# The low part of a gated layer's weights: two 64-row products in the two halves of the array, in groups of two steps

## The chip, the cores and the metric

One core of one Trainium2 chip runs the whole program. The metric is the time of one execution on the device in microseconds; of several executions the median counts. TensorE (PE) multiplies, VectorE (DVE), ScalarE (ACT) and GpSimd (POOL) do the rest on chip, and SyncE (SP) issues most transfers.

## The reference

Three stages follow each other: a gated linear attention, a mixture of eight experts with two experts per token, and a gated dense layer. The change is in the last stage, for 1536 tokens of 320 columns:

```python
def _moe2_ref(x, w_gate, w_val, w_out):
    g = x @ w_gate                                # 320 -> 1536
    silu = g * (1.0 / (1.0 + np.exp(-g)))
    val = x @ w_val                               # 320 -> 1536
    return (silu * val @ w_out).astype(np.float32)   # 1536 -> 320

def reference(**kwargs):
    ...
    attn_out = _attn_ref(**attn_kwargs)
    ...
    x = _moe_ref(x=x, **moe_kwargs)
    return _moe2_ref(x=x, **moe2_kwargs)
```

## The kernel before

The second layer (the last stage) takes the tokens in thirds (`q`, 512 tokens each) and the 1536 hidden columns in twelve steps (`f`, 128 columns each): 36 steps, in the order of the loop at L1105. Numbers are multiplied as float32r, which keeps fewer bits than float32, so each operand is split into a high and a low part and a product is made of three: high by high, high by low, low by high.

The 320 input columns are three pieces: two of 128, and the last of 64. `x2part` transposes the tokens piece by piece (`px`, L834), and makes for the first two pieces the tiles `x2h` (high) and `x2l` (low). The last piece is laid twice into 128 rows, and its tile `xr` (`x2r` in the trace) has the high part in rows 0 to 63 and the low part in rows 64 to 127. The weights' last piece also stands twice in its 128 rows, so one product with `xr` makes high by high and high by low together. The product of the weights' low part with `xr` uses all 128 rows as well.

`passes` (L646) issues the eight matmuls of one sum: three for each of the first two pieces, two for the last. `l1` (L843) calls it twice in each step, for the gate (`pg`) and the value (`pv`), each into a bank of PSUM of its own. The banks come from the ring `A` of four, which `px` uses too. Then ScalarE makes the sigmoid `sg` of `pg` (L852), VectorE multiplies `pg` by `sg` (L853) and that by `pv` (L854) into `u`. `l1_split` splits `u` into `uh` (ScalarE, L862) and `ul` (VectorE, L863). `l2` (L865) multiplies these by the output weights: twelve matmuls of 320 columns per step (L874) into four banks (`py`, rings `Y` and `O`) that sum over the twelve steps of a third; after the last step ScalarE and VectorE take turns in evicting the four banks into tiles `osb`, and SyncE stores them. The `osb` tiles use the buffers of `u` and `sg`, two of each.

The order on each engine is the order of the code. A step is: `l1`; two pieces of weights of the next groups of columns, split by ScalarE (L545) and VectorE (L546), as long as there are any (16 in the first third); in the first third `combine`, in which VectorE adds gathered expert rows (L803) and ScalarE copies the last columns (L798); `l1_split`; `l2` of two steps before (`LAG`); after steps 8, 9 and 10 of the first two thirds one piece of the next third's `x2part`.

Of the kernel before, what the change touches and what calls it, by code (L numbers as in the profile page):

```python
# [7 lines left out]
F32 = mybir.dt.float32  # L8
F32R = mybir.dt.float32r
# [22 lines left out]
CVN = 44  # L32
# attention: chunks after which a batch of tokens is routed, lag of the copies to DRAM and of the first loads
BT = (0, 2, 4, 6, 8, 10, 12)
# [3 lines left out]
XI = 10  # L38
# experts: steps of a unit that prepare the next unit's tokens, units whose sums lie in the other banks,
# step at which the first full unit's tokens are loaded, units whose last columns are doubled on ScalarE  # L40
XK = (4, 5, 6)
OB = (1, 9)
XL = 10
DU = (0, 1, 2)
# columns of the moving operands: heads per product of the attention, columns of the gate's weights
IW = 3
GW = 128
# gathers of expert rows in the last units (CA) and in the second layer's first steps
CA = (1, 1, 1, 1, 1, 1, 1, 2, 1, 1, 0, 0, 0)
XS = 5  # L50
CM2 = (2, 2, 2, 1, 2, 2, 2, 1, 3, 2, 2, 1)
# after the attention: 0 is a step of the experts, k that many steps of the last routing
SEQ = (0, 0, 6, 2, 0, 2, -99)
# pieces of weights that are split per step
RT = (1, 1, 2, 1, 2, 1, 2, 1, 0, 0, 2, 1, 1, 1, 2, 1, 1, 1, 2, 1, 1, 1, 2, 1, 1, 1, 3, 1, 1, 1, 2, 1, 1, 1, 1, 2, 2, 0, 3, 2, 1, 1, 1, 2, 2, 1, 3, 1, 1, 1, 1, 2, 2, 1, 2, 1, 1, 2, 1, 2, 2, 1, 2, 2, 1, 2, 1, 2, 2, 1, 2, 0, 1, 2, 1, 2, 2, 1, 2, 1)
AN = 6
AT = (5,9,7,11)
AG = (5, 11, 8)
# programs of the start, the second, the middle and the last chunks (codes in ON_START and ON_CHUNK;
# in START those of ON_CHUNK are shifted by 256)  # L60
START = 'gffhqkQlffffffff1cfrffff2dffsffffxoOffSffff34WKfTy5Gmfnafwfe6ffffŇŷ7ũŗŋűzųŮŭŶť'
# [29 lines left out]
def kernel(ctx, tc, qk, kvh, og, gates, cst, wgn, noise, w1, w2, w13, w2o, out):  # L91
# [10 lines left out]
    def bankA(name):  # L102
        return ps.tile([128, 512], F32, name=name, tag="A")
# [9 lines left out]

    # ---------------- persistent tiles and constants
    CW = cst.shape[1]
# [40 lines left out]

    # ---------------- attention
    mos = ExitStack()
# [219 lines left out]

    # ---------------- routing
    def route(t0, t1):  # L380
# [124 lines left out]

    # ---------------- weight stream: load, split into two float32r parts
    EX = [(e, 0) for e in SPLIT] + [(e, 0) for e in FULL] + [(e, 1) for e in SPLIT]
# [41 lines left out]

    # ---------------- float64 weights to float32, through DRAM  # L550
    CV = []
# [42 lines left out]

    # ---------------- experts
    XG, XT, HT, YP = {}, {}, {}, {}
# [48 lines left out]

    def passes(ps_ap, wt, wl, cols, xt, n):  # L646
        xh, xl, xr = xt
        seq = []
        for k in range(2):
            c = slice(k * 512 + cols, k * 512 + cols + 128)  # L650
            seq += [(wt[:, c], xh[:, k, 0:n]), (wt[:, c], xl[:, k, 0:n]), (wl[:, c], xh[:, k, 0:n])]
        c = slice(1024 + cols, 1024 + cols + 128)
        seq += [(wt[:, c], xr[:, 0:n]), (wl[:, c], xr[:, 0:n])]
        for i, (a, b) in enumerate(seq):
            pe.matmul(ps_ap, a, b, start=(i == 0), stop=(i == len(seq) - 1))  # L655

# [53 lines left out]

    # ---------------- tokens beyond the capacities
    def overflow_counts():
# [66 lines left out]

    # ---------------- second layer  # L780
    X2 = {}
# [37 lines left out]
    def x2prep(q):  # L819
        pool = m2 if q == 1 else xp[0]  # L820
        xh = pool.tile([128, 2, 512], F32R, name="x2h", bufs=1)
        xl = pool.tile([128, 2, 512], F32R, name="x2l", bufs=1)
        xr = pool.tile([128, 512], F32R, name="x2r", bufs=1)
        X2[q] = (xh, xl, xr)

    def x2part(q, k0, k1):
        if q not in X2:
            x2prep(q)
        xh, xl, xr = X2[q]
        for k in range(k0, k1):  # L830
            ready(q, k)
            p = bankA("px2")
            for a in range(4):
                pe.transpose(p[:, a * 128:(a + 1) * 128], x[:, q * 4 + a, k * 128:(k + 1) * 128], ident)  # L834
            if k < 2:
                s.activation(xh[:, k, :], p, AF.Copy)
                v.tensor_tensor(out=xl[:, k, :], in0=p, in1=xh[:, k, :], op=OP.subtract)
            else:
                s.activation(xr, p, AF.Copy)
                v.tensor_tensor(out=xr[64:128], in0=p[64:128], in1=xr[64:128], op=OP.subtract)  # L840

    UT, OP_ = {}, {}

    def l1(q, f):
        st = GU[f // 4]
        pg = bankA("pg2")
        passes(pg, *WT[st[0]], (f % 4) * 128, X2[q], 512)
        pv = bankA("pv2")
        passes(pv, *WT[st[1]], (f % 4) * 128, X2[q], 512)
        sg = m2.tile([128, 512], F32, name="sg")  # L850
        u = m2.tile([128, 512], F32, name="u")
        s.activation(sg, pg, AF.Sigmoid)  # L852
        v.tensor_tensor(out=sg, in0=pg, in1=sg, op=OP.mult)  # L853
        v.tensor_tensor(out=u, in0=pv, in1=sg, op=OP.mult)  # L854
        UT[q, f] = u

# [8 lines left out]
    def l2(q, f):  # L865
        if f == 0:
            OP_[q] = banksY(4)
        wh, wl = WT[GU[f // 4][2]]
        c = slice((f % 4) * DM, (f % 4 + 1) * DM)
        uh, ul = UT[q, f]  # L870
        for a in range(4):
            t = slice(a * 128, (a + 1) * 128)
            for i, (x_, w) in enumerate(((uh, wh), (uh, wl), (ul, wh))):
                pe.matmul(OP_[q][a][:, 0:DM], x_[:, t], w[:, c], start=(f == 0 and i == 0), stop=(f == 11 and i == 2))  # L874
            if f == 11:
                o = m2.tile([128, 512], F32, name="osb", tag=("u", "sg")[a % 2])[:, 0:DM]
                if a % 2 == 0:
                    s.activation(o, OP_[q][a][:, 0:DM], AF.Copy)
                else:
                    v.tensor_copy(o, OP_[q][a][:, 0:DM])  # L880
                r0 = (q * 4 + a) * 128
                sy.dma_start(out[r0:r0 + 128, :], o)

    # ---------------- experts
    steps = [(n, f) for n in range(len(EX)) for f in range(8)]
# [71 lines left out]

    # ---------------- attention schedule
    def clear():
# [143 lines left out]
    bg = [p for k in (1, 2) for u in GU[k] for p in wpieces(u)]  # L1103
    steps = [(q, f) for q in range(3) for f in range(12)]
    for i, (q, f) in enumerate(steps):  # L1105
        l1(q, f)
        for _ in range(2):
            if bg:
                bg.pop(0)()
        if q == 0:  # L1110
            combine(CM2[f])
        l1_split(q, f)
        if i >= LAG:
            l2(*steps[i - LAG])
        if f in (8, 9, 10) and q < 2:
            x2part(q + 1, f - 8, f - 7)
    for q, f in steps[-LAG:]:
        l2(q, f)

# [64 lines left out]
```

## Time and profile before

| | us |
|---|---|
| median of 3 runs | 567.21 (565.85 to 569.94) |
| profiled execution, span from first to last instruction | 577.4 |
| profiled execution, outside the span | not listed on the page |
| second layer in it, first pg matmul to last py matmul | 375.5 to 573.7 |

The span and all the rows below are of the one profiled execution. The page gives busy times as sums over the whole program; what a stretch is limited by is read from the rows of that stretch, above all from which engine's wait ends last in it.

### The profile page before, as it was taken

Reading aid. Unit: us, or ns where it says so; the run is one execution under the profiler, and the core shown is the slowest. Engines: PE = TensorE matmul, PEld = TensorE weight load, DVE = VectorE, ACT = ScalarE, POOL = GpSimd, SP = SyncE. Lnnn points to the kernel's source line nnn. Section 1 sums busy time; section 2 is a strip of 40 time slices with the busy share of each in tenths; the row PEclk is TensorE's granted clock in tenths of the full one; section 3 lists DMA queues with packets and bytes.
Section 4 is the critical chain, followed back from the end, with each engine's and each line's share of the span. In section 5 each row is a group of like instructions: output and inputs, shape, how many; then the busy total and the mean of one; then the engine's idle time right before and its main releaser. Section 6 shows DMA issues by size and latency. Waiting matters only on the chain. (4 is left out here: it accounts for less than half of the span.)

```text
span 577.4 us, 9288 instructions
## 1 busy us (share of the span) xinstructions
PE 541.0 (94%) x3337; PEld 488.4 (85%) x3337; DVE 383.6 (66%) x884; ACT 276.9 (48%) x599; POOL 176.6 (31%) x207
## 2 busy tenths in 40 slices
PE   8998878859799989999999969999999999999997
PEld 4677878758689979999999969988888888888886
DVE  5447887887558988889989847877753434434433
ACT  5345644323356667778776836555332222222221
POOL 4034666555412735353533315433100000000000
PEclk7559887879979989999999989999999999999999
DMA  8748664402755777888987747744000100010001
GB/s 243 164 139 261 204 210 143 146 23 104 218 197 170 262 266 255 298 300 286 310 306 253 266 162 256 231 151 157 23 2 0 47 1 0 2 45 1 0 1 45
DMA packets 36055, 88.72 MB, mean 154 GB/s; under 512 B 10640, under 2 KB 16944, under 8 KB 36000
## 3 DMA queue, kind: packets, MB, share of 16 engines
q1 hardware_dynamic: 30320, 75.08, 39.5%
q0 software_dynamic: 3360, 8.38, 4.8%
q10 hardware_dynamic: 2320, 4.58, 2.3%
q8 instruction: 28, 0.46, 0.3%
q14 instruction: 27, 0.22, 0.1%
HBM read 72.80 MB, written 15.21 MB: 152 GB/s over the span
## 5 line engine op out<-in xcount | busy, mean ns | idle before, releaser
L692 PE MATMUL py<-wV,h 128*128 128x320 f32 (+1 forms) x624 | 108.5, 315 | 3.1 <-ACT ysb L703 2.3
L692 PEld LDWEIGHTS py<-wV,h 128*128 128x128 f32 (+1 forms) x624 | 97.2, 188 | 4.8 <-ACT ysb L703 2.8
L655 PE MATMUL ph<-xh,wU 128*128 128x416 f32 (+1 forms) x320 | 91.2, 335 | 4.9 <-issue 4.1
L585 POOL TENSOR_TENSOR cq<-cq,csg 128x512 f32<-128x512 f32 (+1 forms) x27 | 39.2, 1453 | 93.0 <-ACT cq L584 60.9
L655 PEld LDWEIGHTS ph<-xh,wU 128*128 128x128 f32 x320 | 59.2, 193 | 7.5 <-issue 4.4
L874 PE MATMUL py<-wV,uh 128*128 128x320 f32 x288 | 63.9, 309 | 0.0
L853 DVE TENSOR_TENSOR sg<-pg,sg 128x512 f32<-128x512 f32 x36 | 24.9, 691 | 58.1 <-ACT sg L852 58.1
L546 DVE TENSOR_TENSOR wU<-stg,wU 128x512 fp32r<-128x512 f32 x72 | 52.4, 753 | 6.2 <-ACT wU L545 5.8
L852 ACT ACTIVATE sg<-pg 128x512 f32<-128x512 f32 x36 | 21.5, 598 | 65.5 <-PE pg L655 60.0
L862 ACT ACTIVATE uh<-u 128x512 fp32r<-128x512 f32 x36 | 22.8, 632 | 61.6 <-DVE u L854 60.7
L655 PE MATMUL ph<-xl,wU 128*128 128x416 f32 (+1 forms) x160 | 52.1, 325 | 0.0
L874 PEld LDWEIGHTS py<-wV,uh 128*128 128x128 f32 x288 | 49.5, 188 | 2.8
L655 PE MATMUL pg<-x2h,wU 128*128 128x512 f32 x144 | 51.2, 396 | 0.0
L655 PE MATMUL pv<-x2h,wU 128*128 128x512 f32 x144 | 50.5, 391 | 0.0
L545 ACT ACTIVATE wU<-stg 128x512 fp32r<-128x512 f32 x78 | 46.4, 624 | 7.0 <-DVE yt L701 4.8
L664 ACT ACTIVATE h<-ph 128x416 fp32r<-128x416 f32 (+1 forms) x80 | 35.7, 447 | 26.2 <-PE ph L655 20.0
L874 PE MATMUL py<-wV,ul 128*128 128x320 f32 x144 | 44.4, 309 | 0.0
L546 DVE TENSOR_TENSOR wV<-stg,wV 128x640 fp32r<-128x640 f32 x42 | 37.0, 890 | 3.5 <-ACT wV L545 3.4
L612 POOL DMA_INDIRECT xgt<-xd,xi x32 | 32.6, 1019 | 21.0 <-PEq L733 6.4
L655 PE MATMUL ph<-xr,wU 128*128 128x416 f32 (+1 forms) x160 | 38.7, 324 | 0.0
L791 POOL DMA_INDIRECT gy<-yg,ig__89 x24 | 25.1, 1046 | 44.0 <-DVE x L803 15.5
L863 DVE TENSOR_TENSOR ul<-u,uh 128x512 fp32r<-128x512 f32 x36 | 24.9, 691 | 19.9 <-ACT uh L862 19.9
(177 smaller groups left out, 1123.7 us busy)
## 6 DMA issues: line engine op xcount, KB each, us to landing
stg<-in_w_dram SPq DMA_DIRECT2D x20, 768.0 KB
stg<-in_w_dram SPq DMA_DIRECT2D x20, 640.0 KB
cw<-in_w_dram SPq DMA_DIRECT2D x18, 512.0 KB
gbt<-gp SPq DMA_DIRECT2D x10, 512.0 KB
f<-cq SPq DMA_DIRECT2D x18, 256.0 KB
stg<-f SPq DMA_DIRECT2D x6, 768.0 KB
kvt<-in_kvh_dram SPq DMA_DIRECT2D x12, 324.0 KB
QK<-in_qk_dram SPq DMA_DIRECT2D x24, 160.0 KB
```

The lines of the kernel that those rows point to most:

```text
L545: s.activation(hi[:, c], ST[u][:, c], AF.Copy)
L546: (g if lo_pool[0] else v).tensor_tensor(out=lo[:, c], in0=ST[u][:, c], in1=hi[:, c], op=OP.subtract)
L585: g.tensor_tensor(out=q, in0=q, in1=sg, op=OP.mult)
L612: g.indirect_dma_start(out=XG[n][0:nr // m, c, 0:DM], out_offset=None, in_=xd[0:S] if n < len(SPLIT) else xd, in_offset=bass.IndirectOffse ...
L655: pe.matmul(ps_ap, a, b, start=(i == 0), stop=(i == len(seq) - 1))
L664: s.activation(h[:, 0:C], p[:, 0:C], AF.Relu)
L692: pe.matmul(yp[0:nr, 0:DM], x_, w, start=st and i == 0, stop=sp and i == 2)
L791: g.indirect_dma_start(out=y, out_offset=None, in_=yg[0:NR0] if j < NC else yg, in_offset=bass.IndirectOffsetOnAxis(ap=ig_[:, j, k:k + 1], ...
L853: v.tensor_tensor(out=sg, in0=pg, in1=sg, op=OP.mult)
L862: s.activation(uh, u, AF.Copy)
L863: v.tensor_tensor(out=ul, in0=u, in1=uh, op=OP.subtract)
L874: pe.matmul(OP_[q][a][:, 0:DM], x_[:, t], w[:, c], start=(f == 0 and i == 0), stop=(f == 11 and i == 2))
```

## The change

Steps are taken in groups of two. `l1` now issues for both steps of a group seven matmuls for `pg` and seven for `pv`, and then four of 64 rows each: for each step the gate's low weights of the last piece, rows 0 to 63, by `xr`'s high part there, and the value's low weights, rows 64 to 127, by the high part in a new tile `xq` (`x2q`), rows 64 to 127. (The product of the low weights by the low part, which the 128 rows also had, is left out.) Only then the sigmoids and products of both steps follow. The group then has four pieces of weights, two calls of `combine`, two of `l1_split`, `l2` of the two steps of the group before, and a piece of `x2part` after the groups that begin with step 6, 8 and 10. `x2part` writes the high part of the last piece twice, into rows 64 to 127 of `xq` and rows 0 to 63 of `xr`. The products of VectorE go into `sg` itself, `u` is gone, and `sg` has three buffers, which the four `osb` tiles use too.

```diff
@@ -643,16 +643,16 @@
                 s.activation(xr[:, 0:C], p[:, 0:C], AF.Copy)
                 v.tensor_tensor(out=xr[64:128, 0:C], in0=p[64:128, 0:C], in1=xr[64:128, 0:C], op=OP.subtract)
 
-    def passes(ps_ap, wt, wl, cols, xt, n):
+    def passes(ps_ap, wt, wl, cols, xt, n, half=False):
         xh, xl, xr = xt
         seq = []
         for k in range(2):
             c = slice(k * 512 + cols, k * 512 + cols + 128)
             seq += [(wt[:, c], xh[:, k, 0:n]), (wt[:, c], xl[:, k, 0:n]), (wl[:, c], xh[:, k, 0:n])]
         c = slice(1024 + cols, 1024 + cols + 128)
-        seq += [(wt[:, c], xr[:, 0:n]), (wl[:, c], xr[:, 0:n])]
+        seq += [(wt[:, c], xr[:, 0:n])] + ([] if half else [(wl[:, c], xr[:, 0:n])])
         for i, (a, b) in enumerate(seq):
-            pe.matmul(ps_ap, a, b, start=(i == 0), stop=(i == len(seq) - 1))
+            pe.matmul(ps_ap, a, b, start=(i == 0), stop=(i == len(seq) - 1 and not half))
 
     def mm1(n, f):
         C, _ = parts(n)
@@ -821,12 +821,13 @@
         xh = pool.tile([128, 2, 512], F32R, name="x2h", bufs=1)
         xl = pool.tile([128, 2, 512], F32R, name="x2l", bufs=1)
         xr = pool.tile([128, 512], F32R, name="x2r", bufs=1)
-        X2[q] = (xh, xl, xr)
+        xq = pool.tile([128, 512], F32R, name="x2q", bufs=1)
+        X2[q] = (xh, xl, xr, xq)
 
     def x2part(q, k0, k1):
         if q not in X2:
             x2prep(q)
-        xh, xl, xr = X2[q]
+        xh, xl, xr, xq = X2[q]
         for k in range(k0, k1):
             ready(q, k)
             p = bankA("px2")
@@ -836,23 +837,30 @@
                 s.activation(xh[:, k, :], p, AF.Copy)
                 v.tensor_tensor(out=xl[:, k, :], in0=p, in1=xh[:, k, :], op=OP.subtract)
             else:
-                s.activation(xr, p, AF.Copy)
-                v.tensor_tensor(out=xr[64:128], in0=p[64:128], in1=xr[64:128], op=OP.subtract)
+                s.activation(xq[64:128], p[64:128], AF.Copy)
+                s.activation(xr[0:64], p[0:64], AF.Copy)
+                v.tensor_tensor(out=xr[64:128], in0=p[64:128], in1=xq[64:128], op=OP.subtract)
 
     UT, OP_ = {}, {}
 
-    def l1(q, f):
-        st = GU[f // 4]
-        pg = bankA("pg2")
-        passes(pg, *WT[st[0]], (f % 4) * 128, X2[q], 512)
-        pv = bankA("pv2")
-        passes(pv, *WT[st[1]], (f % 4) * 128, X2[q], 512)
-        sg = m2.tile([128, 512], F32, name="sg")
-        u = m2.tile([128, 512], F32, name="u")
-        s.activation(sg, pg, AF.Sigmoid)
-        v.tensor_tensor(out=sg, in0=pg, in1=sg, op=OP.mult)
-        v.tensor_tensor(out=u, in0=pv, in1=sg, op=OP.mult)
-        UT[q, f] = u
+    def l1(q, fs):
+        xq, out_ = X2[q], []
+        for f in fs:
+            st = GU[f // 4]
+            pg, pv = bankA("pg2"), bankA("pv2")
+            passes(pg, *WT[st[0]], (f % 4) * 128, xq[0:3], 512, True)
+            passes(pv, *WT[st[1]], (f % 4) * 128, xq[0:3], 512, True)
+            out_.append((f, st, pg, pv))
+        for f, st, pg, pv in out_:
+            c = slice(1024 + (f % 4) * 128, 1024 + (f % 4 + 1) * 128)
+            pe.matmul(pg, WT[st[0]][1][0:64, c], xq[2][0:64, :], start=False, stop=True)
+            pe.matmul(pv, WT[st[1]][1][64:128, c], xq[3][64:128, :], start=False, stop=True)
+        for f, st, pg, pv in out_:
+            sg = m2.tile([128, 512], F32, name="sg", bufs=3)
+            s.activation(sg, pg, AF.Sigmoid)
+            v.tensor_tensor(out=sg, in0=pg, in1=sg, op=OP.mult)
+            v.tensor_tensor(out=sg, in0=pv, in1=sg, op=OP.mult)
+            UT[q, f] = sg
 
     def l1_split(q, f):
         u = UT[q, f]
@@ -873,7 +881,7 @@
             for i, (x_, w) in enumerate(((uh, wh), (uh, wl), (ul, wh))):
                 pe.matmul(OP_[q][a][:, 0:DM], x_[:, t], w[:, c], start=(f == 0 and i == 0), stop=(f == 11 and i == 2))
             if f == 11:
-                o = m2.tile([128, 512], F32, name="osb", tag=("u", "sg")[a % 2])[:, 0:DM]
+                o = m2.tile([128, 512], F32, name="osb", tag="sg", bufs=3)[:, 0:DM]
                 if a % 2 == 0:
                     s.activation(o, OP_[q][a][:, 0:DM], AF.Copy)
                 else:
@@ -1101,21 +1109,26 @@
     m2 = ctx.enter_context(tc.tile_pool(name="m2", bufs=2, side="right", reuse_waits="tile"))
     wu.append(ctx.enter_context(tc.tile_pool(name="wx", bufs=4, side="right", reuse_waits="tile")))
     bg = [p for k in (1, 2) for u in GU[k] for p in wpieces(u)]
-    steps = [(q, f) for q in range(3) for f in range(12)]
+    steps = [(q, f) for q in range(3) for f in range(0, 12, 2)]
     for i, (q, f) in enumerate(steps):
-        l1(q, f)
-        for _ in range(2):
+        l1(q, (f, f + 1))
+        for _ in range(4):
             if bg:
                 bg.pop(0)()
         if q == 0:
             combine(CM2[f])
+            combine(CM2[f + 1])
         l1_split(q, f)
-        if i >= LAG:
-            l2(*steps[i - LAG])
-        if f in (8, 9, 10) and q < 2:
-            x2part(q + 1, f - 8, f - 7)
-    for q, f in steps[-LAG:]:
-        l2(q, f)
+        l1_split(q, f + 1)
+        if i >= 1:
+            a, z = steps[i - 1]
+            l2(a, z)
+            l2(a, z + 1)
+        if f in (6, 8, 10) and q < 2:
+            x2part(q + 1, (f - 6) // 2, (f - 4) // 2)
+    a, z = steps[-1]
+    l2(a, z)
+    l2(a, z + 1)
 
 
 def host_arrays(i):
```

On TensorE, in the third step before and in the second group after (both in the first third), at the end of `l1` and the start of `l2`; the numbers behind `pg` and `pv` tell one bank's use from another, brackets what a row waits for. Before:

```order
L655 MATMUL pv_5385<-x2h,wU 128x512 [waits DVE_49]
L655 MATMUL pv_5385<-x2l,wU 128x512
L655 MATMUL pv_5385<-x2h,wU 128x512 x2
L655 MATMUL pv_5385<-x2l,wU 128x512
L655 MATMUL pv_5385<-x2h,wU 128x512
L655 MATMUL pv_5385<-x2r,wU 128x512 x2
L874 MATMUL py<-wV,uh 128x320 [waits Activation_49]
L874 MATMUL py<-wV,uh 128x320
```

After:

```order
L655 MATMUL pv_5393<-x2l,wU 128x512
L655 MATMUL pv_5393<-x2h,wU 128x512
L655 MATMUL pv_5393<-x2r,wU 128x512
L856 MATMUL pg_5376<-x2r,wU 128x512
L857 MATMUL pv_5377<-x2q,wU 128x512
L856 MATMUL pg_5392<-x2r,wU 128x512
L857 MATMUL pv_5393<-x2q,wU 128x512
L882 MATMUL py<-wV,uh 128x320 [waits Activation_49]
L882 MATMUL py<-wV,uh 128x320
L882 MATMUL py<-wV,ul 128x320 [waits DVE_49]
```

The second `x2r` product of each eight is gone from its place; at the end of the group stand two of L856 and two of L857, and then `l2` of the group before.

On TensorE at the first steps of the layer, where no `l2` stands between. Before, from the second step's value on:

```order
L655 MATMUL pv_5344<-x2h,wU 128x512 [waits PE_49]
L655 MATMUL pv_5344<-x2l,wU 128x512
L655 MATMUL pv_5344<-x2h,wU 128x512 x2
L655 MATMUL pv_5344<-x2l,wU 128x512
L655 MATMUL pv_5344<-x2h,wU 128x512
L655 MATMUL pv_5344<-x2r,wU 128x512 x2
L655 MATMUL pg_5376<-x2h,wU 128x512 [waits DVE_49]
L655 MATMUL pg_5376<-x2l,wU 128x512
```

After, at the end of the first group:

```order
L655 MATMUL pv_5315<-x2h,wU 128x512
L655 MATMUL pv_5315<-x2r,wU 128x512
L856 MATMUL pg_5298<-x2r,wU 128x512
L857 MATMUL pv_5299<-x2q,wU 128x512
L856 MATMUL pg_5314<-x2r,wU 128x512
L857 MATMUL pv_5315<-x2q,wU 128x512
L655 MATMUL pg_5376<-x2h,wU 128x512 [waits DVE_49]
L655 MATMUL pg_5376<-x2l,wU 128x512
```

The first product that waits for VectorE to free a bank was the third step's `pg`; now it is the second group's `pg_5376`, which follows directly on the four halves of the first group.

On VectorE at the end of the program, the last steps' products, splits and evictions. Before:

```order
L853 TENSOR_TENSOR sg<-pg_6782,sg 128x512 [waits Activation_49]
L854 TENSOR_TENSOR u<-pv_6791,sg 128x512 [waits DVE_49,PE_49]
L863 TENSOR_TENSOR ul<-u,uh 128x512 [waits Activation_49]
L853 TENSOR_TENSOR sg<-pg_6821,sg 128x512 [waits Activation_49]
L854 TENSOR_TENSOR u<-pv_6830,sg 128x512 [waits DVE_49,PE_49]
L863 TENSOR_TENSOR ul<-u,uh 128x512 [waits Activation_49]
L880 COPY osb<-py 128x320 [waits PE_49] x2
```

After:

```order
L861 TENSOR_TENSOR sg<-pg_6754,sg 128x512 [waits Activation_49]
L862 TENSOR_TENSOR sg<-pv_6755,sg 128x512 [waits DVE_49,PE_49]
L861 TENSOR_TENSOR sg<-pg_6770,sg 128x512 [waits Activation_49]
L862 TENSOR_TENSOR sg<-pv_6771,sg 128x512 [waits DVE_49,PE_49]
L871 TENSOR_TENSOR ul<-sg,uh 128x512 [waits Activation_49]
L871 TENSOR_TENSOR ul<-sg,uh 128x512 [waits PE_49,Activation_49]
L888 COPY osb<-py 128x320 [waits DVE_49,PE_49]
L888 COPY osb<-py 128x320 [waits DMAHW1_49,PE_49,Activation_49]
```

The four products stand ahead of the two splits, and the last eviction now waits for a transfer (DMAHW1) too.

## Rows read from the trace of the kernel before

**Rows 1.** The page's chain that ended last: engine, output, line, share of the span

```profile
PE pg L655 11%; PE pv L655 11%; PE py L874 11%; PE py L692 3%; PE ph L655 3%; PE px L834 1%; PE py L686 0%; PE pxt L638 0%; DVE osb L880 0%
```

**Rows 2.** The chain in order of time, second layer: start, us, engine, output, line

```profile
499.16 0.44 PE px L834 x4
...
537.43 1.83 PE pg L655 x8
539.26 1.81 PE pv L655 x8
541.07 1.76 PE py L874 x12
...
573.76 0.49 DVE osb L880
```

**Rows 3.** Busy times of the engines over the second layer

```profile
core 0: us, PE busy (x) PEld busy (x) DVE busy (x) ACT busy (x) POOL busy (x), PEclk, DMA share, GB/s
375.50:574.00 198.50, 198.22 (x1034) 173.97 (x1032) 97.06 (x150) 61.43 (x109) 12.19 (x12) 1.00 0.10 31
```

**Rows 4.** Timeline, PE and its weight loads (PEld), attention: start, us

```profile
46.43 1.88 PE L316 MATMUL pY<-kvt,W 128*128 128x123 f32 x16
...
49.48 0.37 PE L279 MATMUL pS<-QK 40*128 40x128 f32 x1
49.69 1.16 PE L279 MATMUL pS<-QK 40*128 40x128 f32 x15
...
49.59 1.07 PEld L279 LDWEIGHTS pS<-QK 40*128 40x128 f32 x15
...
50.78 0.37 PE L301 MATMUL py<-Cb,QK 128*128 128x123 f32 x1
```

**Rows 5.** Timeline, PE, start of the program

```profile
6.50 0.39 PE L253 MATMUL py<-ones 128*128 128x512 bf16 x1
6.82 0.37 PE L238 MATMUL pG<-G__122,ck 16*128 16x128 f32 x1
```

**Rows 6.** Timeline, PE, experts, after a transpose over 32 rows

```profile
192.20 0.46 PE L655 MATMUL ph<-xh,wU 128*128 128x416 f32 x1
192.49 0.35 PE L655 MATMUL ph<-xl,wU 128*128 128x416 f32 x1
```

**Rows 7.** Timeline, PE, ACT and DVE, steps of the first third

```profile
389.54 0.62 PE L655 MATMUL pg<-x2r,wU 128*128 128x512 f32 x2
...
390.20 0.60 ACT L852 ACTIVATE sg<-pg 128x512 f32<-128x512 f32 x1 [1.72 <-PE pg L655]
...
386.32 0.69 DVE L853 TENSOR_TENSOR sg<-pg,sg 128x512 f32<-128x512 f32 x1
387.11 0.69 DVE L854 TENSOR_TENSOR u<-pv,sg 128x512 f32<-128x512 f32 x1
...
390.83 0.69 DVE L853 TENSOR_TENSOR sg<-pg,sg 128x512 f32<-128x512 f32 x1 [0.29 <-ACT sg L852]
```

**Rows 8.** Timeline, DVE, pieces of weights and sums of expert rows there

```profile
387.72 1.28 DVE L546 TENSOR_TENSOR wU<-stg,wU 128x512 fp32r<-128x512 f32 x2
388.92 1.01 DVE L803 SCALAR_TENSOR_TENSOR x<-gy,wn,x 128x320 f32<-128x320 f32 x2
```

**Rows 9.** Timeline, ACT and DVE, the last piece of x2 for the last third

```profile
499.64 0.60 ACT L839 ACTIVATE x2r<-px 128x512 fp32r<-128x512 f32 x1 [0.78 <-PE px L834]
...
500.27 0.69 DVE L840 TENSOR_TENSOR x2r<-px,x2r 64x512 fp32r<-64x512 f32 x1 [0.69 <-ACT x2r L839]
```

**Rows 10.** Timeline, DVE, ACT and SP: evictions and stores of the output

```profile
516.17 0.88 DVE L880 COPY osb<-py 128x320 f32<-128x320 f32 x2
...
454.14 0.60 ACT L852 ACTIVATE sg<-pg 128x512 f32<-128x512 f32 x1 [3.71 <-DMA out_dram<-osb]
...
518.59 0.60 ACT L852 ACTIVATE sg<-pg 128x512 f32<-128x512 f32 x1 [1.82 <-DMA out_dram<-osb]
...
572.49 0.44 ACT L878 ACTIVATE osb<-py 128x320 f32<-128x320 f32 x1 [2.59 <-PE py L874]
...
572.95 1.80 SPq L882 DMA_DIRECT2D out_dram<-osb  x4
```

## The prediction

> **What bounds the kernel now.** I read the page's chain first, then the chain in order of time, then one table of busy times for the second layer. The chain gives a third of the whole span to three lines, the gate product (pg), the value product (pv), both L655, and the output product (py, L874) [rows 1]. In order of time they follow each other without a gap: 1.83 us for eight matmuls of pg, 1.81 for eight of pv, 1.76 for twelve of py [rows 2]. From 375.50 to 574.00 TensorE is busy 198.22 of 198.50 us at a granted clock of 1.00 (the 2.4 GHz level), VectorE 97.06, ScalarE 61.43 [rows 3]. So the second layer is bound by TensorE alone: what is taken off its queue there comes off the time one for one, and every new gap in that queue is paid in full. A pg or pv matmul takes a slot of (1.83 + 1.81) / 16 = 0.228 us [rows 2].
>
> The profiled span is 577.4 us and the median of the three runs 567.21, 10.2 us less. The second layer runs at full clock and without gaps in the profile, so I carry a difference found there over to the median unchanged: 567.21 plus the sum.
>
> **What is taken away.** Each step has 16 matmuls of 512 columns: eight for pg, eight for pv. In each eight the last one multiplies the weights' low part by xr, all 128 rows. After the change its 64 useful rows remain: pg's in the upper half of the array, pv's in the lower. A group of two steps then has 28 full matmuls and four halves. Do two halves run at once? The attention's scores are such products: 40 rows each, at partition 0 and at 64 in turn, into two banks. Fifteen of them take 1.16 us [rows 4], so one starts every (1.16 - 0.27) / 14 = 0.064 us, while products of 123 columns that use all rows start every (1.88 - 0.27) / 15 = 0.107 us [rows 4]. Two halves therefore cost about one full product. I expect the same at 512 columns: two pairs take two slots, and a group saves two of 32 slots, 0.456 us; over 18 groups 8.2 us.
>
> One rule speaks against the second pair. In the scores the fifteen weight loads also take only 1.07 us [rows 4]: two loads per half-pair time, so a load for a half goes on while a product in that same half streams. The Trainium skill's TensorE: Matmul & The Clock Gate, Part 3 (The mechanism), says that a weight load overlaps a running matmul only when its row group differs. By that the second pair, in the same two halves as the first, would wait for its loads, by a load's 0.10 us, and the sum would be 18 x 0.10 = 1.8 us higher, 570.4. The trace disagrees, and I leave it out of the sum.
>
> **What is added: two changes of rows per group.** The array goes from products over 128 rows to products over 64 and back. The trace shows what such a change costs. At 6.50 a full-row product of 512 columns starts; the next, over 16 rows, starts at 6.82, and takes 0.37 us [rows 5], where the same kind without a change takes 0.27 (as 0.37 against 0.27 among the scores [rows 4]). So the next product begins 0.32 us later and then waits 0.10 for weights that could not be loaded ahead: 0.42 in place of a slot of 0.228, so +0.19. Back again: after the last score, which starts at 49.69 + 1.16 - 0.27 = 50.58, the full-row product comes at 50.78 and takes 0.37 [rows 4], 0.20 + 0.10 in place of 0.107: again +0.19. In the experts, after a transpose over 32 rows, L655's first product takes 0.46 and the next, without a change, 0.35 [rows 6]; 0.11 of unhidden load is there for this kernel's own operand type too. Bounds: 0.10 (the load alone) to 0.22 per change; I take 0.19, since the row at 6.50 has the 512 columns. A group: -0.456 + 2 x 0.19 + 0.01 (second half of each pair starts a little later) = -0.066; 18 groups: **-1.2 us** (-4.4 to -0.1). Most of the gain goes into these gaps.
>
> **The first group.** A group holds all four banks of the ring A until its ends, since pg and pv close only with the halves. Between later groups the output product of the group before, 24 matmuls and 2 x 1.76 = 3.52 us [rows 2], covers the eviction. After the first group there is none: the second group's pg follows at once and needs pg's bank. The eviction: pg's last matmul of a step starts at 389.54 + 0.62 - 0.39 = 389.77 and its slot ends at 390.00; the sigmoid starts at 390.20, VectorE's product at 390.83, and the bank is free at 391.52 [rows 7], 1.52 after. With T the end of the last half, the first pg ends one slot earlier, T - 0.23, its bank is free at T + 1.29, and the load makes it T + 1.39. Less the change of rows that is already counted: **+1.2 us** once (0.9 to 1.6).
>
> **The later groups.** After T, VectorE does four products; a product that reads the result of the one before it follows after 0.79 [rows 7], others after 0.61 [rows 7, 8]: T + 0.60, 1.39, 2.00, 2.79, end T + 3.48. Then in the first four groups four pieces of weights (0.64 each), up to four sums of expert rows (0.50 each) [rows 8], and two splits (0.69 like the products): done by about T + 9.5. The next group ends at T + 3.52 + 30 x 0.228 + 0.4 = T + 10.8. VectorE keeps up with 1.3 us to spare; if that cover is gone, the sums and splits queue in front of the next products. The banks are free at T + 1.3 to 3.5 and asked for at T + 3.7 and later. The three buffers for uh and ul ask for one back at T + 1.95, when the earlier step's output product is done, and ScalarE writes it at T + 3.55: no cost.
>
> The loads of weights on SyncE and the gathers on GpSimd (busy 12.19 us in the whole stretch [rows 3]) keep their order; a group's sums take rows that were asked for in the group before, since two of the four gather buffers are always ahead, and the pieces are ready a group before their weights are used: no cost, or the group's length less the 9.5 above, if a transfer came late.
>
> **The hand-over of x2 between the thirds.** The transposes of the last piece now stand directly ahead of the next group. They end at T + 4.15; the product with xr is six slots later, T + 5.52. xr takes ScalarE's copy, 0.48 after the transposes start [rows 2, 9], so T + 4.20 to 4.80, and then VectorE's subtraction of 0.69 [rows 9], T + 5.55. The second ScalarE copy lies beside it. Wait 0.1, twice: **+0.2** (0 to 0.8).
>
> **The end.** The last output product needs its first ul. VectorE has it at T + 4.1, TensorE asks at T + 3.71 + 0.29 = T + 4.0: **+0.15** (0 to 0.5). The four output tiles now share three buffers instead of four, so the fourth eviction waits until the first store has landed. Store landing: the second tile of the middle third is evicted at 516.17 + 0.49 = 516.66 and the sigmoid that needs its buffer starts at 518.59, 1.9 later; in the first third the sigmoid sat 3.71 us for it [rows 10]. At the end the first tile is ready at 572.49 + 0.44 = 572.93, landed at 574.83; the fourth eviction, now at 573.76 [rows 2], starts then, and its store, the last of four issues that take 1.80 us from 572.95 [rows 10], goes out 1.05 later: **+1.05** (0.5 to 2.9). In the two earlier thirds the same wait holds VectorE only, until about T + 7, and nobody asks before T + 10.8.
>
> **Sum:** -1.2 + 1.2 + 0.2 + 0.15 + 1.05 = **+1.4 us, 568.6**. All low ends together -3.0 (564.2), all high ends +5.7 (572.9).
>
> **Rivals.** *The change of rows is free.* Weights are loaded ahead and the halves start in the next slot. Then -8.2, and the single terms are 1.4 + 0.2 + 0.15 + 1.05 = 2.8: -5.4, 561.8. For it: nothing in the trace but that this kernel's only direct pair of a full 512-column product of its type and a 64-row one does not exist yet. Against it: rows 4, 5 and 6 show the gap for three kinds of products. The Trainium skill's TensorEngine Tiling, Theoretical Speedup, gives up to 2x for contractions of 64 rows, which would make this rival's time; its Key Properties say that a change of tiling mode drains the engine, which the trace bears out with 0.19 us. Chance 0.10.
>
> *The halves do not run together.* The four halves (L856, L857) add to sums that already stand in the banks, which the scores do not; if two such products into two banks go one after the other, a group takes 32 slots and the changes on top: +0.456 x 18 = +8.2, 576.8. It decides where a second half starts 0.2 us after its partner instead of within 0.02. Against it: [rows 4]. Chance 0.06.
>
> **How the numbers follow.** The forecast has 0.84. Of it 0.04 lies below 564.0 or above 572.5, where the unknown sizes (price of a change of rows, landing of a store) come together at one end. The range 564.0 to 572.5 leaves out those and both rivals, about 0.2. One per cent, about what a measurement of this kernel can tell from no change, is 5.7 us: under 561.5 lies a little less than half of the first rival and hardly any of the forecast, 0.05; over 572.9 the second rival and the top of the forecast's tail, 0.09; between them 0.86.
>
> **What would show it.** In the changed profile: halves (L856, L857) that start in pairs within 0.02 us; 0.3 from the last full matmul to the first half's load and the same from the last half to py or px, at each of the 18 groups; pg plus pv of two steps in about 7.23 instead of 7.30 us; a wait of about 1.2 us for VectorE at the second group's pg, and none later; the last eviction waiting about 1 us for the first store. It would be wrong if the gaps were missing, if a group stalled for its banks each time, or if the pairs started one slot apart.

## The result, and the profile after

The changed kernel takes a median of 572.45 us (22 runs) against 569.59 for the kernel before beside it (22 runs). Some executions of either kernel run in a slower state; the others give a ratio of 1.0080, 95% interval 1.0056 to 1.0104, or +4.5 us on 567.21 (3.2 to 5.9). I had forecast +1.4.

The profiled execution took 572.81 us with a span of 571.1. That cannot be set against the span of 577.4 before: what runs ahead of the second layer takes 375.5 us there and 365.75 here, and 362 to 374 in the other profiles, though the code ahead is the same but for one ScalarE copy. So from here on the measure is the **second layer**, from the first pg matmul to the start of the last eviction: 198.25 us before (375.51 to 573.76 [rows 2, 3]), **201.90 after** (365.75 to 567.65), +3.65. From the start of the last eviction to the end of the span it is 3.62 us before and 3.46 after, so with what follows the difference is +3.49. Both lie inside the interval of the whole; the 1.0 us up to its middle is not seen in the layer.

The busy times of that stretch (PE, PEld, DVE, ACT, POOL, clock, DMA share, GB/s), and of one group of two steps:

```profile
365.75:567.65 201.90, 198.29 (x1034) 164.13 (x1032) 94.52 (x150) 59.97 (x111) 13.84 (x12) 1.00 0.10 32
385.00:395.74 10.74, 10.74 (x59) 8.99 (x58) 7.96 (x14) 4.61 (x10) 3.45 (x3) 1.00 0.56 182
```

TensorE is at the 2.4 GHz level throughout, as before [rows 3], but 3.6 us of the stretch are now idle. Before it was 0.04; the 0.28 of [rows 3] lie nearly all behind the last product, since that window ends 0.24 us later. The page's chain has the halves (L856) with 2% of the span where [rows 1] had none, and behind them, small, a DMA of the output and VectorE's write of x2r:

```profile
PE py L882 12%; PE pv L655 10%; PE pg L655 10%; PE pg L856 2%; DMA gy<-yg,ig__89 2%; PE py L692 1%; PE ph L655 1%; PE px L835 1%; DMA out_dram<-osb 0%; POOL gy L791 0%; POOL xgt L631 0%; DVE wU L546 0%; DVE x2r L842 0%; ACT x2r L841 0%; ACT x2q L840 0%
```

The chain in order of time (start, us, engine, output, line), one group in the steady part, beside [rows 2]:

```profile
380.78 0.42 PE pg L856
381.21 0.00 PE pv L857
381.21 0.23 PE pg L856
381.44 0.00 PE pv L857
381.44 3.72 PE py L882 x24
385.16 1.60 PE pg L655 x7
...
389.94 1.59 PE pv L655 x7
391.52 0.42 PE pg L856
```

From 380.78 to 391.52 a group takes 10.74 us; two steps took 1.83 + 1.81 + 1.76 twice, 10.80 [rows 2]. The second half of each pair adds 0.00 or 0.01: the halves do run together. But the first pair takes 0.42 in place of a slot of 0.23, and the 24 output products behind them 3.72 in place of 3.52. What the pairs save, the two changes of rows take back, but for 0.06.

The timeline of the first group and what follows it (start, us, engine, line, operation, idle before and who ended it):

```profile
372.21 0.49 PE L856 MATMUL pg<-x2r,wU 64*128 64x512 f32 x1
372.22 0.49 PE L857 MATMUL pv<-x2q,wU 64*128 64x512 f32 x1
372.32 0.19 PEld L856 LDWEIGHTS pg<-x2r,wU 64*128 64x128 f32 x1
...
372.55 0.39 PE L856 MATMUL pg<-x2r,wU 64*128 64x512 f32 x1
372.55 0.39 PE L857 MATMUL pv<-x2q,wU 64*128 64x512 f32 x1
...
372.74 1.09 ACT L860 ACTIVATE sg<-pg 128x512 f32<-128x512 f32 x2 [4.50 <-PE pv L857]
373.37 0.69 DVE L861 TENSOR_TENSOR sg<-pg,sg 128x512 f32<-128x512 f32 x1 [6.80 <-ACT sg L860]
...
374.12 0.50 PE L655 MATMUL pg<-x2h,wU 128*128 128x512 f32 x1 [1.18 <-DVE sg L861]
```

Here TensorE sits 1.18 us for the bank of the first pg, as forecast. It happens once: the other groups have the output products between.

The same view at the end of the first third, where x2's last piece is made just ahead of the group that reads it:

```profile
429.98 0.59 ACT L840 ACTIVATE x2q<-px 64x512 fp32r<-64x512 f32 x1
...
430.59 0.59 ACT L841 ACTIVATE x2r<-px 64x512 fp32r<-64x512 f32 x1
...
430.95 0.39 PE L655 MATMUL pg<-x2h,wU 128*128 128x512 f32 x1
431.21 0.69 DVE L842 TENSOR_TENSOR x2r<-px,x2q 64x512 fp32r<-64x512 f32 x1 [0.61 <-ACT x2r L841]
...
431.96 0.50 PE L655 MATMUL pg<-x2r,wU 128*128 128x512 f32 x1 [0.63 <-DVE x2r L842]
...
432.30 0.40 PE L655 MATMUL pv<-x2h,wU 128*128 128x512 f32 x1
```

The product with xr was due one slot after 430.95, at 431.18, and starts at 431.96. Its successor comes 0.34 later, not 0.23, since its weights are loaded late too. So 0.78 + 0.11 = 0.88 with rounding, and the same again at the end of the second third: **1.76 us**. The row of VectorE shows the cause: its subtraction writes rows 64 to 127 of x2r and waits 0.61 us for ScalarE's copy into rows 0 to 63. (It reads nothing of that copy; that it waits because both write one tile is read from the code, and no run gave them tiles of their own.) The two ScalarE copies and the subtraction stand in a row of three, 0.6 + 0.6 + 0.7.

Three smaller waits, in the timeline of step 9 of the first third, the last output product, and the last evictions:

```profile
411.87 0.19 PEld L655 LDWEIGHTS pv<-x2h,wU 128*128 128x128 f32 x1 [0.32 <-DVE x2l L838]
...
562.98 0.19 PEld L882 LDWEIGHTS py<-wV,ul 128*128 128x128 f32 x1 [0.28 <-DVE ul L871]
...
566.07 0.44 ACT L886 ACTIVATE osb<-py 128x320 f32<-128x320 f32 x1 [0.38 <-PE py L882]
567.65 0.49 DVE L888 COPY osb<-py 128x320 f32<-128x320 f32 x1 [1.53 <-DMA out_dram<-osb]
```

The first is for the bank that px had (0.15 us on TensorE: the chain's seven pv products there take 1.79 in place of 1.64), the second for the last step's ul (0.28), the third for the first store. In the kernel before, the fourth eviction (573.76 [rows 2]) starts 0.44 after ScalarE's second:

```profile
573.32 0.44 ACT L878 ACTIVATE osb<-py 128x320 f32<-128x320 f32 x1 [0.39 <-PE py L874]
```

So it would have come at 566.51, and comes 1.14 later.

Worked out from these rows: 18 x -0.06 = -1.08, +1.18, +1.76, +0.15, +0.28, +1.14: **+3.43** of the 3.65. About 0.2 stays unplaced; the experiments put 0.08 of it on the first group and 0.04 on the last eviction.

### The profile page after: what moved, and what is told of

It reads as the page before. It is cut to its first block, busy times and chain, and to the rows that moved or that the text cites. A ratio compares the mean times of both kernels' runs of the same rounds, so it can differ in the third digit from the quotient of the medians.

```text
span 571.1 us, 9340 instructions
## 1 busy us (share of the span) xinstructions
PE 532.7 (93%) x3337; PEld 472.2 (83%) x3337; DVE 381.9 (67%) x884; ACT 276.0 (48%) x602; POOL 177.4 (31%) x207
## 5 line engine op out<-in xcount | busy, mean ns | idle before, releaser
L860 ACT ACTIVATE sg<-pg 128x512 f32<-128x512 f32 x36 | 19.6, 596 | 102.4 <-PE pv L857 96.0
L882 PE MATMUL py<-wV,uh 128*128 128x320 f32 x288 | 65.4, 315 | 0.0
L882 PEld LDWEIGHTS py<-wV,uh 128*128 128x128 f32 x288 | 47.5, 187 | 6.2 <-issue 6.2
L870 ACT ACTIVATE uh<-sg 128x512 fp32r<-128x512 f32 x36 | 22.3, 630 | 26.4 <-DVE sg L862 26.4
L545 ACT ACTIVATE wV<-stg 128x640 fp32r<-128x640 f32 x46 | 33.1, 732 | 1.9 <-DVE yt L701 1.9
```

The costliest lines, as they stand in the source:

```text
L545: s.activation(hi[:, c], ST[u][:, c], AF.Copy)
L870: s.activation(uh, u, AF.Copy)
```

## The experiments

My theory: the halves run together, two changes of rows take the gain back, and single waits (first group, hand-over of x2, last store) make the kernel slower. Rivals: the halves do not pair; the changes are free and something else costs; the waits only show where VectorE and ScalarE are too late anyway. All lengths below are of the second layer, against 201.90 after and 198.25 before, and each is of one profiled execution; the wait of the first group, where its code is unchanged, is 1.17 or 1.18 in each. Whole times of single runs (568.60 to 581.15) are not compared, since the part ahead of the layer, 362 to 374 us, differs more than most edits do. The runs of the kernel before beside them took 565.37 us (first four), 567.06 (next three) and a median of 567.37 (last two).

**Whole copy first.** xr is copied whole and the subtraction follows it, as in the kernel before; xq comes last.

```diff
-                s.activation(xq[64:128], p[64:128], AF.Copy)
-                s.activation(xr[0:64], p[0:64], AF.Copy)
-                v.tensor_tensor(out=xr[64:128], in0=p[64:128], in1=xq[64:128], op=OP.subtract)
+                s.activation(xr, p, AF.Copy)
+                v.tensor_tensor(out=xr[64:128], in0=p[64:128], in1=xr[64:128], op=OP.subtract)
+                s.activation(xq[64:128], p[64:128], AF.Copy)
```

> Second layer = from the first pg matmul to the start of the last eviction: 198.25 us before, 201.90 after. Here ScalarE writes xr whole first, VectorE subtracts after that copy alone, and ScalarE fills xq later. Theory (the hand-over of x2 waits for ScalarE's second copy): each of the two hand-overs 0.6 us shorter, second layer 200.7. Rival (the product with xr waits because ScalarE and VectorE are late with the splits ahead of the copies): no change, 201.9.

Measured: 200.71. Two thirds of the 1.76 are gone. What is left is seen in its chain, same place:

```profile
434.40 0.64 ACT uh L870
...
435.07 0.69 DVE ul L871
...
435.79 0.70 DVE x2r L841
...
436.54 0.50 PE pg L655
```

The subtraction now stands behind the group's own products and splits on VectorE. So the copy's order was the larger part of the wait, and the place of x2part right after a group's work the rest (the last experiment but one moves it).

**A fourth output buffer.** The last osb tile of a third uses a buffer of uh.

```diff
-                o = m2.tile([128, 512], F32, name="osb", tag="sg", bufs=3)[:, 0:DM]
+                o = m2.tile([128, 512], F32, name="osb", tag="uh" if a == 3 else "sg", bufs=3)[:, 0:DM]
```

> The fourth output tile takes a buffer of uh in place of one of the three of sg. Theory (the last eviction waits for the first store to land): the wait of about 1.1 us is gone, second layer 200.8. Rival (the last eviction is late for another reason, the late ul or the store queue): 201.9.

Measured: 200.72, -1.18. The last eviction in its timeline waits for the output product only, as in the kernel before [rows 2]:

```profile
563.27 0.49 DVE L888 COPY osb<-py 128x320 f32<-128x320 f32 x1 [0.39 <-PE py L882]
```

**First group as two of one step.**

```diff
-        l1(q, (f, f + 1))
+        if i == 0:
+            l1(q, (f,))
+            l1(q, (f + 1,))
+        else:
+            l1(q, (f, f + 1))
```

> The first group is taken as two groups of one step. Theory (its banks are closed too late, and nothing covers the eviction): the stall of 1.25 goes, two more changes of rows come, 0.38: second layer 201.05. Rival (the wait for banks only moves to the next group): 201.9 or more.

Measured: 201.03. In its chain the next pg follows the pair at once, with a long first slot in the 1.82 and no wait:

```profile
369.35 0.43 PE pg L856
369.78 0.00 PE pv L857
369.78 1.82 PE pg L655 x7
```

It pays one more pair of changes of rows (about 0.39) and saves 0.87, so the stall was worth 1.26: the idle time and the weight load that is late with it.

**Groups without halves.** Whole eights as before, everything else of the change.

```diff
-            passes(pg, *WT[st[0]], (f % 4) * 128, xq[0:3], 512, True)
-            passes(pv, *WT[st[1]], (f % 4) * 128, xq[0:3], 512, True)
+            passes(pg, *WT[st[0]], (f % 4) * 128, xq[0:3], 512)
+            passes(pv, *WT[st[1]], (f % 4) * 128, xq[0:3], 512)
...
-            pe.matmul(pg, WT[st[0]][1][0:64, c], xq[2][0:64, :], start=False, stop=True)
-            pe.matmul(pv, WT[st[1]][1][64:128, c], xq[3][64:128, :], start=False, stop=True)
```

> Groups of two as in the changed kernel, but eight whole products for each pg and pv, and no halves. Theory (halves and changes of rows nearly cancel; the loss is in the waits that the grouping makes): 18 x 0.06 = 1.1 more in the products, the first stall (1.25) and the late ul (0.28) gone, hand-over and last store as they are: 201.45, that is 3.2 over before without any half. Rival (the changes of rows cost more than they give and make the loss): back to about 198.25.

Measured: 201.22, 2.97 above the kernel before without one half-array product in it. Its timeline has the hand-over as it was, and the last eviction waits for the store as after:

```profile
436.77 0.69 DVE L842 TENSOR_TENSOR x2r<-px,x2q 64x512 fp32r<-64x512 f32 x1 [2.21 <-ACT x2r L841]
...
437.52 0.73 PE L655 MATMUL pg<-x2r,wU 128*128 128x512 f32 x2 [0.62 <-DVE x2r L842]
...
573.61 0.49 DVE L884 COPY osb<-py 128x320 f32<-128x320 f32 x1 [1.51 <-DMA out_dram<-osb]
```

The loss comes from the grouping, with the new copies of x2 directly ahead of their reader, and from the buffers, not from the halves. It lies 0.23 under my figure; 0.15 of that is the wait for px's bank, which does not come up here.

**Halves in every step.** One step per group, in the old order with its lag of two steps: one pair and two changes of rows per step.

```diff
-    steps = [(q, f) for q in range(3) for f in range(0, 12, 2)]
+    steps = [(q, f) for q in range(3) for f in range(12)]
...
-        l1(q, (f, f + 1))
+        l1(q, (f,))
...
```

> Halves as in the changed kernel, but step by step in the order of before (one step per group, lag 2). Theory (a change of rows costs 0.19, a pair of halves saves 0.228): per step 0.16 more than before, 36 x 0.16 = 5.8, the last store 1.1, no other wait: second layer 205.1 where before had 198.25. Rival (changes of rows are nearly free): 36 x 0.228 = 8.2 less, 191.

Measured: 205.75. Two lines of its chain, one step:

```profile
395.52 0.43 PE pg L856
395.95 0.00 PE pv L857
395.95 1.96 PE py L882 x12
...
401.11 0.43 PE pg L856
```

A step takes 5.59 in place of 5.40 [rows 2]: a pair saves 0.23, two changes cost 0.42. That the changes are free is refuted. The layer is 0.65 above my figure: less the store's 1.14 it is 0.18 a step over all 36, where I had counted 0.16. One pair between two changes pays 0.42 here and two pairs paid 0.39 above, so the price hangs on the change and not on the number of halves.

**All four halves in the same rows.** The value's halves use rows 0 to 63 too (the weights' last piece stands twice in its rows, so the sums are the same).

```diff
-            pe.matmul(pv, WT[st[1]][1][64:128, c], xq[3][64:128, :], start=False, stop=True)
+            pe.matmul(pv, WT[st[1]][1][0:64, c], xq[2][0:64, :], start=False, stop=True)
```

> All four 64-row products of a group in the upper half of the array (gate's and value's, both by xr). Theory (two run at once only because they lie in different halves): two slots more per group, 18 x 0.456 = 8.2, second layer 210.1, and halves that start 0.23 apart. Rival (64-row products overlap wherever they lie): 201.9.

Measured: 209.35. Its halves in the timeline:

```profile
373.09 0.49 PE L856 MATMUL pg<-x2r,wU 64*128 64x512 f32 x1
...
373.43 0.39 PE L857 MATMUL pv<-x2r,wU 64*128 64x512 f32 x1
...
373.66 0.39 PE L856 MATMUL pg<-x2r,wU 64*128 64x512 f32 x1
...
373.89 0.39 PE L857 MATMUL pv<-x2r,wU 64*128 64x512 f32 x1
```

Now each half takes a slot: 64-row products run together only in different rows. A steady group takes 11.22, 0.48 more than after, the two slots that the pairs save; the total is 0.75 below what I expected, since the halves' longer time covers 0.47 of the first group's wait (0.71 us idle in place of 1.18) and all of the last ul's. The third and fourth start 0.23 apart though each needs its own weights in rows that are streaming. So the 0.34 between the first two, here and between the two pairs of the changed kernel, belongs to the change of rows. The Trainium skill's TensorE: Matmul & The Clock Gate, Part 3 (The mechanism), says that a weight load overlaps a running product only in another row group (though it also names a background weight buffer). By that rule alone the third and fourth would also be about 0.34 apart, an estimate from 373.09 and 373.43. The trace disagrees with it.

**No change of rows.** In place of four halves, two products over all 128 rows, one into a pg and one into a pv bank (half of the products of the weights' low part with the last piece are left out): the same two slots, no change of rows.

```diff
...
-            pe.matmul(pg, WT[st[0]][1][0:64, c], xq[2][0:64, :], start=False, stop=True)
-            pe.matmul(pv, WT[st[1]][1][64:128, c], xq[3][64:128, :], start=False, stop=True)
+            if f % 2 == 0:
+                pe.matmul(pg, WT[st[0]][1][:, c], xq[2], start=False, stop=True)
+            else:
+                pe.matmul(pv, WT[st[1]][1][:, c], xq[2], start=False, stop=True)
```

> In place of the four 64-row products a group has two of 128 rows, one into one step's pg and one into the other's pv; half of the products of the weights' low part with the last piece are left out. As many slots as with overlapped halves, but no change of rows. Theory (two changes of 0.19 per group): 18 x 0.38 = 6.9 less, second layer 195.0. Rival (the gaps around the halves are the price of the halves themselves, not of changing): 201.9.

Measured: 195.88. Its chain:

```profile
388.88 0.23 PE pg L857
389.10 0.23 PE pv L859
389.33 3.52 PE py L884 x24
...
399.24 0.23 PE pg L857
```

A group takes 10.36, 0.38 less than after: 0.19 in the first half's place (0.42 to 0.23), 0.20 in the output products (3.72 to 3.52). Over 18 groups that is 6.8, and the layer is 6.02 shorter; the other 0.8 went into longer waits, which the shorter groups no longer cover: 1.78 us of idle at the two hand-overs in place of 1.25, the rest for px's bank and the last ul.

**x2 one group earlier.** Of the changed kernel only the place of x2part is moved.

```diff
-        if f in (6, 8, 10) and q < 2:
-            x2part(q + 1, (f - 6) // 2, (f - 4) // 2)
+        if f == 8 and q < 2:
+            x2part(q + 1, 0, 3)
```

> The changed kernel with one edit: the three pieces of x2 for the next third are made after the group of step 8, one group earlier than before, nothing else. My theory: the two hand-overs of 0.88 us and the 0.15 us wait for px's bank go, and the second layer takes 201.90 - 1.76 - 0.15 = 200.0 us. Rival (the same work only waits elsewhere, on VectorE's queue or for a bank): 201.9 us.

Measured: 199.81. Twelve transposes stand behind the output products, and the next pg follows with no wait:

```profile
416.12 3.72 PE py L882 x24
419.83 1.31 PE px L835 x12
421.14 1.64 PE pg L655 x7
```

All 1.76 + 0.15 are gone, with the copies in the slow order; the layer is 2.09 shorter, and the 0.18 beyond that were not followed up. So the place alone makes or removes the wait, and the order of the copies is two thirds of its length.

**All waits gone.** Halves in 16 groups, whole eights in the first and the last, the copy order of the first experiment, the fourth buffer, and x2 one group earlier.

```diff
...
-        l1(q, (f, f + 1))
+        l1(q, (f, f + 1), 0 < i < len(steps) - 1)
...
```

> The changed kernel with the waits it adds taken away together: first and last group with whole eights in place of halves (no stall at the start, and the last step's ul is not waited for), halves in the other 16 groups, the whole copy of x2's last piece ahead of the split, all three pieces of x2 made one group earlier, and the fourth output tile in another buffer. My theory: only the halves' net gain is left, 16 x 0.06 = 1.0 us, so the second layer takes about 197.25 us (197.0 to 198.0) against 198.25 before, and the whole run is about 0.998 of before, which timing can hardly tell from 1. Rival (VectorE and ScalarE have no room, and the waits come back elsewhere): 198.3 us or more, ratio 1.000 to 1.004.

Measured: 197.25. That it fits to the digit is luck, since the 0.06 of a group is read to 0.01, or 0.16 over 16 groups. The whole run takes 566.65 us (12 runs) against 567.37, ratio 0.9978 (0.9946 to 1.0010), which timing does not tell from no change. Its chain at the end is TensorE alone up to the last eviction:

```profile
554.47 1.87 PE pv L655 x8
556.33 7.06 PE py L882 x48
...
563.41 0.49 DVE osb L888
```

The mechanism of the change is worth 1.0 us of the second layer here, and what was lost were the waits.

## Why the prediction was wrong in size

- **Halves run together: right.** Pairs start 0.00 to 0.01 apart; in the same rows they take a slot each. The 8.2 us are really saved on the array.
- **Two changes of rows per group at 0.19: right.** 0.19 in, 0.20 out, 0.38 together without them. The group's -0.06 was forecast as -0.066. The prices read at 6.50 and among the scores [rows 4, 5] held for this operand type and 512 columns (0.21 with halves in every step); the rival that the change is free falls with the runs of halves in every step and of no change of rows. The Trainium skill's TensorEngine Tiling (Array Packing), Key Properties, says that a change of tiling mode drains the engine. These runs agree, with 0.19 to 0.21 us a change. The Trainium skill's TensorEngine Tiling (Array Packing), Theoretical Speedup, gives up to 2x where the small dimension is 64 or less. That holds for the pair alone, not for a group, whose net gain is 0.06 of the 0.456.
- **First group, +1.2: right** (1.18 idle, 1.26 by the experiment). **Later groups, nothing: right**, but for 0.15 where a bank was still px's, which I had left out since I took the banks of pg and pv alone.
- **Hand-over of x2, +0.2: this step failed.** Its sum of times has one ScalarE copy and the subtraction, and of the other copy it says: "The second ScalarE copy lies beside it." It does not: VectorE's subtraction sits 0.61 us until that copy has ended, and the late product then opens a weight load, 0.11, that I had not counted either. The two hand-overs cost 0.88 each in place of 0.1, 1.76 in all. The upper bound I gave, 0.8, did not take in that wait; before the change the piece was made one step ahead with a whole step's products between, so the trace of before shows nothing of it.
- **Late ul, +0.15: 0.28.** The wait was 0.18, and the load that then lies open 0.10: I counted the wait alone.
- **Fourth eviction, +1.05: right** (1.14; 1.18 by the experiment, of which what follows the eviction gives 0.16 back).
- **Carrying the second layer's difference over to the whole: borne out** as far as it can be, +3.65 within 3.2 to 5.9.

With the hand-over at its measured 1.76 the forecast's sum would have been +3.0, beside the 3.2 at the lower end of the measured interval: of the 2.25 us by which the second layer missed the forecast, one chain of three short operations made 1.56. It did not settle the sign: with that wait gone (x2 one group earlier) the layer is still 1.56 longer than before.

## What to carry to other kernels

Before products are packed into halves of the array, count the changes of shape they bring: here each costs nearly as much as the slot that a pair saves (0.19 to 0.21 against 0.23), so one pair between two changes loses 0.19 and two gain 0.06, and the number of open banks sets how many can. When work is moved directly ahead of its reader, write out the chain of its operations by engine, and treat two writers of one tile as a chain even where they write different rows. Longer groups also hold buffers longer: look for the place without cover (first group, last stores).

## What the runs showed of the hardware

The price of a change of rows is about 0.2 us wherever it could be read, for unlike products: from a bf16 one to one over 16 rows [rows 5], from the scores of 40 rows back to all rows [rows 4], and both ways for this kernel's 64 rows. Of it 0.10 is a weight load that is not hidden (0.34 between two starts in place of 0.23); what the other 0.1 is made of stays open, as no run separated it.

Not looked for: in f = 8 to 11 of the first and last third, eight pg or pv products take 1.87 us in place of 1.82 in the kernel before and in the run with all waits gone (above, at 554.47), and seven take 1.64 in place of 1.59 in the changed kernel, at the same granted clock of 1.00, and not in the middle third. I did not test why.
